# Router's logits and ranks in PSUM, branch sums behind the last scatter, expert 0's rows on two queues

## The chip, the cores and the metric

The kernel runs on one core of a Trainium2 chip. The metric is the device time of one execution in microseconds (us), from the kernel's start to its end; three runs of the kernel before are given. A core has TensorE (PE, matmuls), VectorE (DVE), ScalarE (ACT), GpSimd (POOL) and SyncE (SP, which here only issues DMAs). Each engine works through its own list of instructions in order and waits on semaphores of the others. DMAs are issued by SP, by ACT and, for the scattered writes, by POOL.

## The reference

Three layers follow each other, all in float32:

```python
# 1. recurrence over 768 steps, 4 x 8 heads, a 40 x 40 state each
y[t]  = r[t] @ state
Sa    = state @ a[t]
state = state * w[t] - outer(Sa, b[t]) + outer(v[t], k[t])
# 2. x = y as 3072 tokens x 320; each token goes to one of 8 experts
logits = x @ w_gate;  e = argmax(logits)
out[e-tokens] = gate * sigmoid(x @ w_output_gate)[e] * (relu(x @ w1[e]) @ w2[e])
# 3. dense: (relu(x @ w_in) ** 2) @ w_out, 320 -> 2048 -> 320
```

## The kernel before

**Stage 1, up to about 445 us.** The recurrence is cut into 24 chunks of 32 steps (128 tokens each, since 4 batches go together). A chunk passes through small stages (`A_scan` to `F_3`), and a table written out by hand (`ORDER`, with `HEAD` and `TAIL` for the first and last chunks) says in which order the stages of neighbouring chunks are issued. The engines therefore work on several chunks at a time, each in the fixed order of that table.

The last three stages of a chunk are the router. `F_1` transposes the chunk's tokens `xs`. `F_2` (`r_oh`, L884) multiplies them with the gate weights: PE writes the logits `lg` to PSUM (L887), ACT copies them behind the tokens in `xs` (L889), and DVE makes a one-hot row of the winning expert in five small instructions: the largest logit `mx` (L891), `val` = rank numbers of the logits that reach it (L893), the largest rank `mv` (L895), the one-hot `oh` (L897), and a copy of two token numbers into `xs` (L898). `F_3` (`r_pos`, L907) counts with two matmuls (`rk`) how many tokens each expert had so far, makes the row number `POS` out of it, and POOL scatters the rows of `xs` to `xsD` in DRAM, where each expert has a region (L920).

Behind the router of a chunk, DVE's next instruction in the order is `B_ev` (L520), a transpose of `LM`, a PSUM tile that PE fills in `B_lm` (L511). POOL meanwhile multiplies in `A_bd` (L497), `A_at` (L484) and `A_recip` (L474), all with two operands in SBUF.

**The branch.** With the last chunk, `beyond` (L901) makes a number in three DVE instructions: whether any expert has more tokens than the main path takes. All engines read it and branch (L1147, L1148); on these inputs the branch jumps over a fallback.

**Stage 2, from about 449 us.** For each expert `load_x` brings 512 of its rows as four blocks of 128 x 402 numbers (201 KB each). For expert 0 SP issues the blocks one by one (L1345) in the order 1, 2, 3, 0, and then expert 1's four blocks as one DMA of 804 KB (L1342). Block 0's rows and half of block 1's were used already, from a copy taken ahead, so `trans_x(0)` lets PE transpose only blocks 1, 2, 3, in this order (L1038). ACT and DVE split the result in two float32r parts (L1023 to L1027), and the matmuls of expert 0 begin (L1033). ACT runs a table load and one dummy activation at the start of the stage (L1358), so that `Exp` is at hand. The rows of block 0 are needed by ACT's copy of the logits of expert 0 (L1396).

**Stage 3, from about 671 us,** is the dense layer on all tokens, bound by matmuls throughout.

Of the kernel before, what the change touches and what calls it, by code (L numbers as in the profile page):

```python
# [20 lines left out]
NCH = S // T  # L21
# [817 lines left out]
def program(tc, A, out, nch=NCH, order=ORDER):  # L839
    nc = tc.nc  # L840
    V, G, S_, P = nc.vector, nc.gpsimd, nc.scalar, nc.tensor
    with ExitStack() as top:
# [39 lines left out]
            return xT  # L882

        def r_oh(c, xs, xT, pm):  # L884
            lg = pm([128, 16], "lg")
            for k in range(3):
                P.matmul(lg, xT[:, k], wg[:, k], start=(k == 0), stop=(k == 2))  # L887
            L = xs[:, 384:392]
            S_.activation(xs[:, 384:400], lg, AF.Copy)  # L889
            mx = rp.tile([128, 1], F32, name="mx")  # L890
            V.tensor_reduce(out=mx, in_=L, axis=AX.X, op=ALU.max)  # L891
            val = rp.tile([128, 8], F32, name="val")
            V.scalar_tensor_tensor(out=val, in0=L, scalar=mx, in1=cst[:, C_DESC : C_DESC + 8], op0=ALU.is_ge, op1=ALU.mult)  # L893
            mv = rp.tile([128, 1], F32, name="mv")
            V.tensor_reduce(out=mv, in_=val, axis=AX.X, op=ALU.max)  # L895
            oh = rp.tile([128, 8], F32R, name="oh")
            V.tensor_scalar(out=oh, in0=val, scalar1=mv, scalar2=None, op0=ALU.is_equal)  # L897
            V.tensor_copy(xs[:, 400:402], cst[:, C_TID + c : C_TID + c + 2])  # L898
            return oh

        def beyond():  # L901

            V.tensor_tensor(out=pv, in0=base[0:1], in1=cst[0:1, C_CAP : C_CAP + 8], op=ALU.subtract)
            V.tensor_reduce(out=fl[:, 0:1], in_=pv, axis=AX.X, op=ALU.max)
            V.scalar_tensor_tensor(out=fi[:, 1:2], in0=fl[:, 0:1], scalar=fl[:, 2:3], in1=fl[:, 1:2], op0=ALU.max, op1=ALU.max)

        def r_pos(c, xs, oh, pm):  # L907
            rk = pm([128, 16], "rk")
            for k in range(2):
                P.matmul(rk[:, 8 * k : 8 * k + 8], cnt[:, k], oh, start=True, stop=True)  # L910
            t = rp.tile([128, 8], F32, name="t")
            V.tensor_tensor(out=t, in0=rk[:, 0:8], in1=base, op=ALU.add)
            V.tensor_tensor(out=t, in0=t, in1=oh.bitcast(F32), op=ALU.mult)
            V.tensor_tensor(out=base, in0=rk[:, 8:16], in1=base, op=ALU.add)
            if c == NCH - 1:
                beyond()
            pf = rp.tile([128, 1], F32, name="pf")
            V.tensor_reduce(out=pf, in_=t, axis=AX.X, op=ALU.add)
            V.tensor_scalar(out=POS[:, c : c + 1], in0=pf, scalar1=0.0, scalar2=E * RS - 1.0, op0=ALU.max, op1=ALU.min)
            G.indirect_dma_start(out=xsD, out_offset=IndirectOffsetOnAxis(ap=POS[:, c : c + 1], axis=0), in_=xs, in_offset=None)  # L920

        def parts(ring, n):
            return [ring[:, 6144 * k : 6144 * k + n].bitcast(F32R) for k in range(2)]
# [410 lines left out]
        with ExitStack() as ctx:  # L1334
# [4 lines left out]
            def load_x(e):  # L1339
                t = xg[e] = xp.tile([128, 4, XW], F32, name="xg", bufs=2)  # L1340
                if e:
                    nc.sync.dma_start(out=t, in_=xsD[e * RS : e * RS + 512].rearrange("(j p) x->p j x", p=128))  # L1342
                else:
                    for j in (1, 2, 3, 0):
                        nc.sync.dma_start(out=t[:, j], in_=xsD[128 * j : 128 * j + 128])  # L1345

            def trans_x(e, ks):
                js = range(4) if e else range(1, 4)
# [7 lines left out]

            with tc.manual_schedule():
                S_.activation(fl[:, 0:1], cst[0:1, 0:1], AF.Exp)  # L1358
                load_x(0)
                load_x(1)  # L1360
                drain(first_w[0])
                trans_x(0, range(3))
                narrow = Narrow()

# [198 lines left out]
```

## Time and profile before

| | us |
|---|---|
| runs | 1009.38, 1016.93, 1022.97 (median 1016.93) |
| profiled execution, its own time | 1027.06 |
| its span, first to last instruction | 1025.3 |
| busy in the span: PE, DVE, ACT, POOL | 940.5 (92%), 684.3 (67%), 613.5 (60%), 464.1 (45%) |
| mean granted TensorE clock | 0.968 |

The profiled execution took 4 us more than the longest of the three runs. Busy shares are means over three stages with different limits, so they are read by stage. A row of a group gives line, engine, operation, tiles, count, then busy time and the mean of one, then the idle time ahead of it and what ended it. A row of a timeline gives the start in us, the length in us, the instruction, and in brackets the idle time of the engine just before.

### The profile page before, as it was taken

To read this page: it belongs to the slowest core of one execution; us is meant where nothing else is said; L and a number is where in the kernel's file an instruction comes from. 1 tells how busy PE (TensorE), PEld (TensorE's weight loads), DVE (VectorE), ACT (ScalarE), POOL (GpSimd) and SP (SyncE) were. 2 spreads that over 40 slices of the span, in tenths; PEclk is the share of its full clock that TensorE was granted. 3 is DMA by queue.
4 is the path that set the end of the run, shared out by engine and by line. 5 is a ranking of instruction groups with operands and counts; after the bars stand their busy time and mean duration, and the time that the engine had idled before them with its cause. 6 is when DMAs were issued, how large, how long until landed. Compare 5 with 4: busy or idle time off the path is not lost.

```text
span 1025.3 us, 33164 instructions
## 1 busy us (share of the span) xinstructions
PE 940.5 (92%) x13845; PEld 833.5 (81%) x13845; DVE 684.3 (67%) x1752; ACT 613.5 (60%) x1366; POOL 464.1 (45%) x449
## 2 busy tenths in 40 slices
PE   1779898999989988889999999999999999999997
PEld 1568677777777777779999999989999989999986
DVE  5879999999989987335777777686444343434341
ACT  4579888897989988435555555545434333344432
POOL 5567777866777775217666666630100101010101
PEclk9889999999999999579999999999999999999999
DMA  3874535444354445327788887773001010000000
GB/s 101 245 215 109 135 103 134 113 115 125 104 143 118 110 126 135 104 97 220 233 258 257 237 240 206 222 165 97 20 8 37 21 31 26 1 26 1 17 10 27
DMA packets 59307, 120.25 MB, mean 117 GB/s; under 512 B 14609, under 2 KB 32145, under 8 KB 57233
## 3 DMA queue, kind: packets, MB, share of 16 engines
q1 hardware_dynamic: 51424, 103.09, 36.6%
q0 software_dynamic: 2688, 8.88, 2.4%
q10 hardware_dynamic: 5040, 6.12, 1.8%
q8 instruction: 110, 1.80, 0.8%
q14 instruction: 45, 0.36, 0.1%
HBM read 92.01 MB, written 26.05 MB: 115 GB/s over the span
## 4 chain that ended last, share of the span: by engine, by line
PE 72%; DVE 14%; issue 5%; ACT 4%; DMA 4%; POOL 1%; POOLq 0%; SPq 0%; DVEq 0%; ACTq 0%
PE ph L1033 27%; PE py L1434 9%; PE po L1291 5%; PE po L1292 5%; PE po L1290 5%; PE tp L707 2%; PE kt L554 2%; PE sc L726 2%; PE ST L670 2%; PE y L754 2%; DMA arena<-in_xE_dram 2%; PE LM L511 1%; PE zt L717 1%; PE lg L887 1%; DVE CB L763 1%
## 5 line engine op out<-in xcount | busy, mean ns | idle before, releaser
L1033 PE MATMUL ph<-x,ring 128*128 128x512 f32 (+2 forms) x1280 | 299.7, 382 | 0.2 <-ACT x L1023 0.2
L1033 PEld LDWEIGHTS ph<-x,ring 128*128 128x128 f32 x1280 | 233.5, 191 | 33.3 <-ACT x L1023 0.6
L1513 POOL DMA_INDIRECT out_dram<-hf,TID x24 | 25.6, 1067 | 309.2 <-ACT hf L1511 268.2
L936 POOL TENSOR_TENSOR ring<-raws,ring 128x732 fp32r<-128x732 f32 (+2 forms) x72 | 124.3, 1741 | 49.4 <-ACT ring L935 42.7
L1484 DVE TENSOR_TENSOR hf<-hf 128x512 f32<-128x512 f32 x96 | 68.6, 714 | 114.2 <-ACT hf L1483 114.0
L1483 ACT ACTIVATE hf<-ph 128x512 f32<-128x512 f32 x96 | 57.3, 596 | 118.4 <-PE ph L1033 118.3
L497 POOL TENSOR_TENSOR arena<-arena 40x1024 f32<-40x1024 f32 x43 | 104.9, 2440 | 40.8 <-DMA hz<-in_vS_dram 13.2
L1291 PE MATMUL po<-ring,hf 128*128 128x320 f32 x368 | 113.6, 309 | 0.8 <-DVE hf L1486 0.8
L1292 PE MATMUL po<-ring,hf 128*128 128x320 f32 x368 | 113.4, 308 | 0.3 <-DVE ring L1311 0.3
L1290 PE MATMUL po<-ring,hf 128*128 128x320 f32 x368 | 113.7, 309 | 0.0
L1486 DVE TENSOR_TENSOR hf<-hf,hf 128x512 fp32r<-128x512 f32 x92 | 64.6, 702 | 64.2 <-ACT hf L1485 64.2
L1434 PE MATMUL py<-hr,ring 128*128 128x448 f32 x512 | 105.3, 365 | 0.0
L1485 ACT ACTIVATE hf<-hf 128x512 fp32r<-128x512 f32 x92 | 58.2, 632 | 76.9 <-DVE hf L1484 76.9
L1434 PEld LDWEIGHTS py<-hr,ring 128*128 128x128 f32 x512 | 95.6, 188 | 7.1
L1043 DVE SCALAR_TENSOR_TENSOR hr<-ph,hr 128x448 fp32r<-128x448 f32 (+2 forms) x72 | 41.1, 571 | 55.7 <-ACT hr L1042 55.4
L1291 PEld LDWEIGHTS po<-ring,hf 128*128 128x128 f32 x368 | 69.1, 188 | 5.1 <-DVE hf L1486 1.3
L1290 PEld LDWEIGHTS po<-ring,hf 128*128 128x128 f32 x368 | 69.0, 188 | 4.5 <-ACT hf L1485 0.4
L1292 PEld LDWEIGHTS po<-ring,hf 128*128 128x128 f32 x368 | 69.0, 187 | 0.6 <-DVE ring L1311 0.6
L935 ACT ACTIVATE ring<-raws 128x732 fp32r<-128x732 f32 (+2 forms) x72 | 57.0, 791 | 8.8 <-DMA raws<-in_we_dram 8.5
L1042 ACT ACTIVATE hr<-ph 128x448 fp32r<-128x448 f32 (+2 forms) x72 | 36.1, 501 | 39.8 <-PE ph L1033 39.8
L1274 POOL TENSOR_TENSOR c<-c,r 128x384 int32<-128x384 int32 (+1 forms) x32 | 35.2, 1100 | 54.3 <-PE ph L1033 10.4
L557 ACT ACTIVATE kSB<-kt,cst 128x320 f32<-128x320 f32 x96 | 45.1, 521 | 13.6 <-PE kt L554 13.3
(217 smaller groups left out, 1987.2 us busy)
## 6 DMA issues: line engine op xcount, KB each, us to landing
raws<-in_we_dram SPq DMA_DIRECT2D x48, 366.0 KB
arena<-in_xE_dram SPq DMA_DIRECT2D x48, 322.5 KB
xL<-in_xL_dram SPq DMA_DIRECT2D x24, 480.0 KB
xsD<-raws SPq DMA_DIRECT2D x24, 268.0 KB
q<-in_wi_dram SPq DMA_DIRECT2D x16, 384.0 KB
xg<-xsD SPq DMA_DIRECT2D x7, 804.0 KB
q<-in_wo_dram SPq DMA_DIRECT2D x16, 320.0 KB
wb<-in_wB_dram SPq DMA_DIRECT2D x24, 165.0 KB
```

What stands on the lines that cost most here:

```text
L497: (V if c < EARLY[2 + hh] else G).tensor_tensor(out=bd[sl, :, :, hh].rearrange("p a b c l j->p (a b) c (l j)"), in0=s["bk"][sl].rearrange( ...
L935: S_.activation(hi, rw, AF.Copy)
L936: G.tensor_tensor(out=lo, in0=rw, in1=hi.bitcast(F32), op=ALU.subtract)
L1033: P.matmul(ps, t[:, o : o + 128], x3[:, i, c], start=(j == 0), stop=(j == 7))
L1290: P.matmul(ps, hh, whi[:, o : o + 320], start=start, stop=False)
L1291: P.matmul(ps, hl, whi[:, o : o + 320], start=False, stop=False)
L1292: P.matmul(ps, hh, wlo[:, o : o + 320], start=False, stop=stop)
L1434: P.matmul(py, w, x, start=(f == 0 and k == 0), stop=last)
L1483: S_.activation(r, ph, AF.Relu)
L1484: V.tensor_tensor(out=q, in0=r, in1=r, op=ALU.mult)
L1485: S_.activation(hh, q, AF.Copy)
L1486: V.tensor_tensor(out=hl, in0=q, in1=hh.bitcast(F32), op=ALU.subtract)
```

## The change

Three edits, the third of them in two places.

```diff
         def r_oh(c, xs, xT, pm):
-            lg = pm([128, 16], "lg")
+            both = pm([128, 24], "lg")
+            lg, val, L = both[:, 0:16], both[:, 16:24], both[:, 0:8]
...
-            L = xs[:, 384:392]
             S_.activation(xs[:, 384:400], lg, AF.Copy)
...
-            val = rp.tile([128, 8], F32, name="val")
             V.scalar_tensor_tensor(out=val, in0=L, scalar=mx, in1=cst[:, C_DESC : C_DESC + 8], op0=ALU.is_ge, op1=ALU.mult)
...
             V.tensor_tensor(out=base, in0=rk[:, 8:16], in1=base, op=ALU.add)
-            if c == NCH - 1:
-                beyond()
...
             G.indirect_dma_start(out=xsD, out_offset=IndirectOffsetOnAxis(ap=POS[:, c : c + 1], axis=0), in_=xs, in_offset=None)
+            if c == NCH - 1:
+                beyond()
...
-                    for j in (1, 2, 3, 0):
-                        nc.sync.dma_start(out=t[:, j], in_=xsD[128 * j : 128 * j + 128])
+                    for j, q in ((2, nc.sync), (3, nc.scalar), (1, nc.sync), (0, nc.scalar)):
+                        q.dma_start(out=t[:, j], in_=xsD[128 * j : 128 * j + 128])
...
                 S_.activation(fl[:, 0:1], cst[0:1, 0:1], AF.Exp)
+                drain(first_w[0])
                 load_x(0)
                 load_x(1)
-                drain(first_w[0])
```

**Router.** The logits that DVE reads and the ranks `val` now lie in one PSUM tile; ACT's copy into `xs` stays. This is DVE's router of one chunk with its waits, before:

```order
L891 TENSOR_REDUCE mx<-xs 128x1 [waits Activation_49]
L893 SCALAR_TENSOR_TENSOR val<-xs,mx,cst 128x8 [waits DVE_49]
L895 TENSOR_REDUCE mv<-val 128x1 [waits DVE_49]
L897 TENSOR_SCALAR oh<-val,mv 128x8 [waits DVE_49]
L898 COPY xs<-cst 128x2
L520 STREAM_TRANSPOSE LB<-LM 128x1024 [waits PE_49]
```

and after:

```order
L891 TENSOR_REDUCE mx<-lg 128x1 [waits Activation_49]
L892 SCALAR_TENSOR_TENSOR lg<-lg,mx,cst 128x8 [waits DVE_49,PE_49]
L894 TENSOR_REDUCE mv<-lg 128x1 [waits DVE_49]
L896 TENSOR_SCALAR oh<-lg,mv 128x8 [waits DVE_49]
L897 COPY xs<-cst 128x2
L520 STREAM_TRANSPOSE LB<-LM 128x1024 [waits PE_49]
```

The order is the same; `val` (now part of `lg`) reads one operand and writes its result in PSUM, `oh` reads PSUM, and the first instruction waits for ACT as before.

**Branch sums.** DVE at the last chunk, from the use of `rk` on, before (L903 to L905 are `beyond`, L1113 and L1114 a sum that stage 2 needs):

```order
L914 TENSOR_TENSOR base<-rk,base 128x8
L903 TENSOR_TENSOR p_86<-base,cst 1x8
L1113 TENSOR_TENSOR p_84<-base,cst 1x8
L904 TENSOR_REDUCE fl<-p_86 1x1
L1114 SCALAR_TENSOR_TENSOR p_85<-p_87,p_85,p_84 1x8
L905 SCALAR_TENSOR_TENSOR fi<-fl 1x1
L918 TENSOR_REDUCE pf<-t 128x1
L919 TENSOR_SCALAR POS<-pf 128x1
```

and after:

```order
L913 TENSOR_TENSOR base<-rk,base 128x8
L915 TENSOR_REDUCE pf<-t 128x1
L1112 TENSOR_TENSOR p_84<-base,cst 1x8
L916 TENSOR_SCALAR POS<-pf 128x1
L902 TENSOR_TENSOR p_86<-base,cst 1x8
L1113 SCALAR_TENSOR_TENSOR p_85<-p_87,p_85,p_84 1x8
L903 TENSOR_REDUCE fl<-p_86 1x1
L904 SCALAR_TENSOR_TENSOR fi<-fl 1x1
```

`POS`, on which the last scatter waits, comes ahead of the three instructions of `beyond` and of one of the other two.

**Expert 0's rows.** ACT at the start of stage 2, before:

```order
L1358 ACT_TABLE_LOAD
L1358 ACTIVATE fl<-cst 1x1
L1023 ACTIVATE x_12288<-pk 128x320 x2
L1026 ACTIVATE x_12288<-pk 128x320
L1396 ACTIVATE gl<-xg 128x72
```

and after:

```order
L1357 ACT_TABLE_LOAD
L1357 ACTIVATE fl<-cst 1x1
L1344 DMA xg<-xsD 128x402 x2
L1022 ACTIVATE x_12240<-pk 128x320 x2
L1025 ACTIVATE x_12240<-pk 128x320
L1395 ACTIVATE gl<-xg 128x72
```

ACT issues blocks 3 and 0 behind its table load; SP is left with blocks 2 and 1, in this order, and expert 1's DMA follows as its third instead of its fifth. The moved `drain` has nothing left to issue: no weight piece of expert 0 stands there in either kernel.

## Rows read from the trace of the kernel before

**Rows 1.** The page: granted clock in 40 slices of 25.6 us, tenths.

```profile
PEclk9889999999999999579999999999999999999999
```

**Rows 2.** Busy time in one stretch: PE, PEld, DVE, ACT, POOL, clock, DMA.

```profile
70.00:400.00 330.00, 296.18 (x9335) 252.61 (x9337) 303.67 (x1021) 287.40 (x735) 240.46 (x267) 0.98 0.44 116
```

**Rows 3.** Waits, 70 to 400 us: total us, times, longest.

```profile
DVE xs L782 <- PE y L754: 13.6, 10, 3.1
...
DVE mx L891 <- ACT xs L889: 3.6, 8, 1.1
```

**Rows 4.** DVE's groups of instructions, 70 to 400 us.

```profile
L893 DVE SCALAR_TENSOR_TENSOR val<-xs,mx,cst 128x8 f32<-128x8 f32 x20 | 11.2, 560 | 0.7
L897 DVE TENSOR_SCALAR oh<-val,mv 128x8 fp32r<-128x8 f32 x20 | 10.8, 542 | 0.7
```

**Rows 5.** Single lines, 70 to 400 us: shortest/median/longest in ns, first and last start.

```profile
L566 DVE TENSOR_SCALAR ST<-Hb,cst x42: 229/236/244, 76.2 to 394.9; 128x16 f32<-128x16 f32 x42
L893 DVE SCALAR_TENSOR_TENSOR val<-xs,mx,cst x20: 225/508/1243, 82.7 to 386.8; 128x8 f32<-128x8 f32 x20
L897 DVE TENSOR_SCALAR oh<-val,mv x20: 231/232/1032, 83.1 to 387.2; 128x8 fp32r<-128x8 f32 x20
L898 DVE COPY xs<-cst x20: 154/160/165, 83.3 to 387.4; 128x2 f32<-128x2 f32 x20
```

**Rows 6.** DVE's timeline at one chunk, 95 to 101.5 us.

```profile
98.10 1.06 DVE L893 SCALAR_TENSOR_TENSOR val<-xs,mx,cst 128x8 f32<-128x8 f32 x1
...
99.39 0.92 DVE L897 TENSOR_SCALAR oh<-val,mv 128x8 fp32r<-128x8 f32 x1
...
100.30 1.24 DVE L520 STREAM_TRANSPOSE LB<-LM 128x1024 f32<-128x1024 f32 x1
```

**Rows 7.** POOL's timeline at the same place.

```profile
97.94 1.19 POOL L484 TENSOR_TENSOR at<-arena,Cx 104x512 f32<-104x512 f32 x1
99.10 1.18 POOL L474 TENSOR_TENSOR arena<-Cx,arena 104x512 f32<-104x512 f32 x1
```

**Rows 8.** PE's timeline at the same place.

```profile
97.92 1.08 PE L511 MATMUL LM<-arena,at 104*32 104x128 f32 x32
```

**Rows 9.** DVE and PE at another chunk, 352.5 to 357 us.

```profile
355.48 1.23 DVE L520 STREAM_TRANSPOSE LB<-LM 128x1024 f32<-128x1024 f32 x1
...
353.56 1.08 PE L511 MATMUL LM<-arena,at 104*32 104x128 f32 x32
```

**Rows 10.** DVE's timeline at the last chunk.

```profile
442.84 0.16 DVE L914 TENSOR_TENSOR base<-rk,base 128x8 f32<-128x8 f32 x1
...
443.57 0.14 DVE L918 TENSOR_REDUCE pf<-t 128x1 f32<-128x8 f32 x1
```

**Rows 11.** Waits of SP's queue, 430 to 470 us.

```profile
SPq L1345 <- DMA xsD<-xs,POS: 3.1, 1, 3.1
...
SPq L1345 <- ACT hr L1042: 0.2, 1, 0.2
```

**Rows 12.** Timeline of SP, ACT and PE behind the branch.

```profile
448.86 1.77 SPq L1345 DMA_DIRECT2D xg<-xsD  x4
...
449.76 1.28 ACT L1358 ACT_TABLE_LOAD   x1 [0.79 <-ACTq L1148]
...
451.46 0.52 PE L1038 MATMUL pk<-cst,xg 128*128 128x128 f32 x3 [2.90 <-DMA xg<-xsD]
...
453.89 0.90 PE L1038 MATMUL pk<-cst,xg 128*128 128x128 f32 x3 [0.96 <-DMA xg<-xsD]
...
454.94 1.32 PE L1033 MATMUL ph<-x,ring 128*128 128x256 f32 x4 [0.16 <-ACT x L1023]
```

**Rows 13.** ACT's queue at its first split: waits, shortest/median/longest ns, first and last start.

```profile
L1023 ACTq EVENT_SEMAPHORE  x3: 17/38/4027, 431.9 to 450.4; - x3
```

**Rows 14.** Stretches of 2 us, columns as in Rows 2.

```profile
454.00:456.00 2.00, 1.84 (x7) 1.42 (x8) 1.04 (x3) 1.26 (x4) 0.00 (x0) 0.50 0.82 294
...
460.00:462.00 2.00, 2.00 (x16) 2.00 (x16) 0.36 (x1) 1.41 (x5) 1.87 (x2) 0.84 0.00 0
```

## The prediction

> **What bounds the kernel now.** I read the page first, for the granted clock in slices: it is 5 and 7 tenths in the two slices from 410 to 461 us and near full elsewhere [rows 1]. So this execution lost time around the end of stage 1, where the change works too. Next I read the busy times of stage 1 without its ends. In 330 us PE is busy for 296, DVE for 304, ACT for 287 [rows 2]: DVE has 26 us of slack, or about 1.3 us in each of the 20 chunks of that stretch. In the waits the reader is to see that DVE's idle time is mostly a wait for PE's `y` ahead of `xs` (13.6 us, 10 times), and that the router's `mx` waits for ACT's copy in 8 chunks (3.6 us) [rows 3]. So DVE and PE take turns: in about half of the chunks DVE comes late, in the others PE.
>
> Then I read the two router instructions by themselves. `val` and `oh` handle 8 numbers per partition, and their shortest cases take 225 and 231 ns; but they go up to 1243 and 1032 ns [rows 5], and 20 of each take 11.2 and 10.8 us [rows 4]. The two timelines show why: `val` starts at 98.10, just after POOL's L484 (97.94), and ends at 99.16, 0.03 us behind that one's end; `oh` starts inside L474 and ends at 100.31, again 0.03 us behind it [rows 6, 7]. DVE is held until POOL is done. The tensor_scalar L566, which writes PSUM, never is (229 to 244 ns in 42 cases) [rows 5].
>
> Last I read the branch. From 449 to 455 us PE has almost nothing to do: it waits for block 1 (till 451.46) and for block 3 (till 453.89), and the first matmul of expert 0 is at 454.94 [rows 12].
>
> **The router's five instructions.** The change takes `val` to PSUM as source and target, and lets `oh` read PSUM; I take both at their shortest, 225 and 231 ns, as L566 has it. In the chunk of rows 6 this saves 1.06 + 0.92 - 0.46 = 1.52 us. But the next instruction on DVE, the transpose of `LM` at 100.30, can't start before PE has `LM`, which ends at 97.92 + 1.08 = 99.00 [rows 8]: no more than 1.30 us come through. At 355.48 the same difference to PE's 353.56 + 1.08 is 0.84 [rows 9]. I took the smaller of the two, saving and distance to `LM`, in each of the 20 chunks: ten have something to give (rows 6 and rows 9 are the first and the last of them), 7.0 us together. The other ten have no held instruction, or `LM` is later than the router. Of the ten, DVE waits for `y` later in the same turn in four, and I take it that their 2.4 us only lengthen this wait. Six are left, with 1.30, 0.56, 0.65, 0.25, 0.97 and 0.84: **-4.6 us**. The end to the fast side is 7.0, with the other four. To the other side, a DVE that runs earlier may meet POOL at another of its two-operand instructions, which costs up to a whole POOL instruction each time (1.2 us [rows 7]); three such meetings eat 3.6 of the 4.6, and I put the end at +1 us.
>
> The copy on ACT stays, and `mx` waits for ACT still, as the order with its waits shows; so the 3.6 us of rows 3 stay too. The PSUM tile is now held until `oh` has read it, but PE's next use of its place is the `rk` of the same chunk or later, which needs `oh` anyway: nothing. PSUM operands for `mx` and `mv` cost nothing I can see.
>
> A rule of the Trainium skill speaks against a part of this. Its page "SBUF — State Buffer", section "SBUF: two separate sides", says that DVE and GpSimd share a pair of ports under an exclusive lock, which a DVE instruction asks for if it has two SBUF inputs or runs in a two-port mode, and that a float32 copy from SBUF to SBUF is of the second kind; `val` and `oh` held to POOL's end agree with it. By it `xs`'s copy of two token numbers, now first to come with operands in SBUF alone, would be held in their place, and the sum would be that of the first rival below.
>
> **The branch sums.** Before, the sum behind `base` (L914, 442.84) starts at 443.57, 0.73 us later, with `beyond` and a scan between [rows 10]. Now one short instruction stays between, so `POS` and the scatter come about 0.6 us earlier. SP's first load of block rows waits for the landed scatter (3.1 us), and behind that 0.2 us for ACT's last early activation [rows 11]; ACT doesn't end earlier, so of 0.6 us at most these 0.2 matter less. I take -0.1, with ends at 0 and -0.6, the whole step, which counts where PE's early matmuls end well ahead of the scatter. The branch's number comes perhaps 0.3 us later; SP reads it first and then stands 3.1 us at the scatter [rows 11]: nothing.
>
> **Expert 0's rows.** Before, SP issues four blocks in 1.77 us from 448.86, 0.44 each, and expert 1's four blocks behind them; block 1 is with PE at 451.46, 2.2 us after its issue ended at 449.3; block 3, third, at 453.89 [rows 12], while 294 GB/s flow [rows 14]. Now SP issues 2, 1 and expert 1's 804 KB; ACT issues 3 and 0. When does ACT come to it? Its table load runs from 449.76 to 451.04 [rows 12], but its queue stood in the last wait ahead of the first split at 450.4 already [rows 13], past the load and the dummy activation. So a DMA at this place goes out at about 450.4, a little later than on SP before (third, by 450.2). Best case: it is served as block 1 was, 450.4 + 0.44 + 2.2 = 453.0, a gain of 0.9. Worst case: it comes last of 8 x 206 = 1,650 KB, which at 294 GB/s take 5.6 us from 449.3, and with the 1.5 us that block 1 took beyond its own 0.7 it is there at 456.4, 2.5 us later. Its nearest row is its own before: block 3 with two blocks in front and expert 1's rows about. I take 0, and keep -0.9 and +2.5. Block 1 is now second on SP, some 0.7 us later (206 KB at 294 GB/s); its three transposes fit into the wait for block 3. Block 0, last on ACT, is needed by ACT's `gl`, which stands behind the splits that wait for block 3; issued 0.44 us behind block 3, with 0.7 us of transfer, it can hold ACT's first activation of expert 0 by about 1 us, while that one waits for eight matmuls first: nothing.
>
> TensorE's clock is at its lower level, 1.2 GHz, from about 454 to 461 us (0.50 in 454 to 456, 0.84 in 460 to 462) [rows 14], after PE had idled; I leave this as it is.
>
> **The sum.** -4.6 - 0.1 + 0 = -4.7 us. The profiled execution took 1027.06 and would take 1022.4. It is 10 us above the median of the runs, 1016.93, for which I forecast 1016.93 - 4.7 = **1012.2 us**.
>
> **The rivals.** (1) *The hold is handed on.* The two-number copy behind `oh` is held instead. For it: its neighbour `oh`, with one SBUF input, is held. Against: 154 to 165 ns in all 20 cases [rows 5], though always right behind an instruction that had waited. In the chunk of rows 6 it would end with L484 at 99.13, little lost; over the six chunks 3.4 of the 4.6 us are left. 1016.93 - 3.5 = 1013.4.
>
> (2) *All of it comes back.* PE or ACT is the bound in these chunks too (90% and 87% busy [rows 2]), and what DVE gains turns into longer waits for `LM` and `y`. Only the branch is left: 1016.8.
>
> (3) *More than the sum.* All ten chunks pass on their share (7.0), the scatter its 0.6, block 3 its 0.9, and PE starts early enough that the low stretch of the clock behind the branch (7 us at half speed, so 3.4 us) doesn't come: -11.9, 1005.0.
>
> (4) *Slower: block 3 behind expert 1's rows.* SP's large DMA now goes out about one us earlier and ahead of block 3, which ACT issues behind a table load. If it is served first, block 3 is there 2.5 us later, and if PE's longer wait brings the clock one more low stretch of 7 us, another 3.4: +5.9, against the router's -4.6 net +1.2, 1018.1. It decides from a block 3 that is 1.3 us late with the longer low clock. For it: the four blocks and the large DMA share the same engines at 82% [rows 14]. Against: block 3 was slowed by this DMA before as well. On this the page "ScalarE: Activation LUTs", section "What ACT_TABLE_LOAD costs", of the Trainium skill says that a load is followed by a drain of 1380 ns; by that ACT would issue at 449.76 + 2.66 = 452.4 and block 3 come at 455.0, 1.1 us late. The queue that waits at 450.4 [rows 13] speaks against it.
>
> **How the numbers follow.** Chances: forecast 0.40, (1) 0.17, (2) 0.20, (3) 0.08, (4) 0.15. All lie within 2% of the median (996.6 to 1037.3), which is about what a measurement of this kernel can tell from no change: its own three runs spread over 1.3%. The clock may explain such a spread: the two low slices of rows 1 make some 40 us at half speed, 7 of them behind the branch, and the other 34 cost up to 17 us. So the range is that of the cases, 1005 to 1018, opened by what the median of a few such runs may be off, about 4 us to either side: 1001 to 1022. Faster by over 2% would need four times the sum: 0.04. Slower by over 2%: 0.02.
>
> **What would show it.** `val` and `oh` near 230 ns in all chunks, and the copy behind them still at 160 (forecast) or up to 1.2 us (1). DVE's waits for `LM` and for `y` (13.6 us before [rows 3]) grown: the more, the more of (2). The scatter's issue about 0.6 us closer to `rk`. ACT's two DMAs at 450.4 relative to a table load at 449.8, and block 3's landing against the first matmul of expert 0: later than 4.8 us after SP's first load means (4). The forecast is wrong if stage 1 from the second to the twentieth chunk isn't shorter by 3 to 6 us.

## The result, and the profile after

The change is slower by 0.8%: 1028.66 us in the median of 20 runs (1020.30 to 1042.28) against 1019.94 for the kernel before in 20 runs, a ratio of 1.0083 with a 95% interval of 1.0060 to 1.0106. The forecast was 4.7 us faster, 1012.2 us from the 1016.93 of three runs; with more runs the kernel before itself stands 3.0 us higher. Measured twice more, on two chips (e5 and h1 below), the change came to 1.0038 (1.0005 to 1.0071) and 1.0102 (1.0065 to 1.0139).

The profiled execution took 1021.77 us (span 1020.0, mean granted clock 0.977). Both profiled executions are poor samples: that of before (1027.06) is above the median of its kernel, that of after far below its own. So the two are compared stretch by stretch, and only where the granted clock is alike.

**Router.** The windows and waits of 70 to 400 us, as [rows 2, 3]; a row of waits gives the total, the times and the longest:

```profile
70.00:400.00 330.00, 301.85 (x9419) 256.67 (x9420) 294.45 (x1027) 291.57 (x743) 244.10 (x266) 0.99 0.44 118
```

```profile
DVE xs L782 <- PE y L754: 19.4, 20, 2.3
DVE LB L520 <- PE LM L511: 3.2, 7, 1.3
DVE mx L891 <- ACT xs L889: 2.7, 5, 1.2
```

DVE is busy for 294 us where it was busy for 304, and now waits for `y` in 20 chunks where it waited in 10: what DVE gained is in part waiting time. The three instructions, as [rows 5] (shortest, median and longest in ns):

```profile
L892 DVE SCALAR_TENSOR_TENSOR lg<-lg,mx,cst x24: 233/234/235, 83.4 to 429.7; 128x8 f32<-128x8 f32 x24
L896 DVE TENSOR_SCALAR oh<-lg,mv x24: 226/226/227, 83.8 to 430.1; 128x8 fp32r<-128x8 f32 x24
L897 DVE COPY xs<-cst x24: 158/160/1049, 84.0 to 430.3; 128x2 f32<-128x2 f32 x24
```

`val` and `oh` are never held any more. The copy behind them now is, up to 1049 ns. Here is that case, DVE's timeline and POOL's:

```profile
192.97 0.23 DVE L896 TENSOR_SCALAR oh<-lg,mv 128x8 fp32r<-128x8 f32 x1
193.11 1.05 DVE L897 COPY xs<-cst 128x2 f32<-128x2 f32 x1
194.08 1.24 DVE L520 STREAM_TRANSPOSE LB<-LM 128x1024 f32<-128x1024 f32 x1
```

```profile
192.96 1.18 POOL L474 TENSOR_TENSOR arena<-Cx,arena 104x512 f32<-104x512 f32 x1
```

The copy ends at 194.16, 0.02 us behind POOL's L474, just as `val` and `oh` did in [rows 6, 7].

**Expert 0's rows.** SP, ACT and PE behind the branch, as [rows 12]:

```profile
437.80 0.91 SPq L1344 DMA_DIRECT2D xg<-xsD  x2
438.75 0.43 SPq L1341 DMA_DIRECT2D xg<-xsD  x1
```

```profile
439.11 1.28 ACT L1357 ACT_TABLE_LOAD   x1 [0.79 <-ACTq L1147]
439.74 1.46 ACTq L1344 DMA_DIRECT2D xg<-xsD  x2
```

```profile
440.95 0.85 PE L1037 MATMUL pk<-cst,xg 128*128 128x128 f32 x6 [3.06 <-DMA xg<-xsD]
444.90 0.90 PE L1037 MATMUL pk<-cst,xg 128*128 128x128 f32 x3 [3.10 <-DMA xg<-xsD]
445.96 0.79 PE L1032 MATMUL ph<-x,ring 128*128 128x256 f32 x2 [0.15 <-ACT x L1022]
```

ACT issues its two blocks 0.63 us after its table load began, one us behind SP's 804 KB. Block 3 comes to PE 7.1 us after SP's first load (before: 5.0), and the first matmul 8.16 us after it (before: 6.08). Stretches of 2 us show when:

```profile
442.00:444.00 2.00, 0.00 (x0) 0.00 (x0) 0.00 (x0) 0.00 (x0) 0.00 (x0) 0.77 1.00 343
444.00:446.00 2.00, 0.94 (x4) 0.55 (x4) 0.06 (x1) 0.53 (x2) 0.00 (x0) 0.50 0.26 94
```

All 16 DMA engines are busy until 444, and block 3 comes as they fall idle: it was among the last of 1,650 KB. The packets of the DMA queues show the order; q1 takes what SP issued, q10 what ACT issued. From 437.8 to 442.6 us (the first line) q10 moved nothing, though ACT had issued at 439.74; from 442.6 to 445 (the other two) its blocks came:

```profile
q1 hardware_dynamic: 631, 0.96, 69.3%
```

```profile
q10 hardware_dynamic: 254, 0.36, 44.4%
q1 hardware_dynamic: 175, 0.26, 29.8%
```

A row gives packets, MB and the share of the 16 engines: of the 1.2 MB that SP issued, 0.96 went out ahead of ACT's first packet.

**The last scatter.** `POS` now comes 0.6 us sooner behind `rk`, as forecast, but the scatter doesn't. POOL's queue waits for `POS` with a semaphore instruction (shortest, median and longest in ns, then its start). Before and after, and the `POS` of after:

```profile
L920 POOLq EVENT_SEMAPHORE  x1: 521/521/521, 443.4 to 443.4; - x1
```

```profile
L917 POOLq EVENT_SEMAPHORE  x1: 43/43/43, 433.1 to 433.1; - x1
432.48 0.15 DVE L916 TENSOR_SCALAR POS<-pf 128x1 int32<-128x1 f32 x1
```

Before, POOL's queue stood there for half a us. After, it came there half a us behind the end of `POS` and went straight on. Now POOL's queue itself comes last, 2.97 us after it began its scatter of the chunk before (2.76 in the kernel before). In all traces of this text that distance is 2.6 to 3.0 us, and only in the trace of before did the queue stand there for `POS`: in e2, e3 and e6 below, which lack this edit, it came last as well. What holds it in this time, the traces don't tell.

**What nobody had touched.** The experts' matmuls stand in the same order with the same operands, and yet they take longer. First the stretches from the first `py` to the first `po` and from there to the end, of before and then of after:

```profile
466.46:674.50 208.04, 208.04 (x1059) 191.79 (x1058) 152.18 (x287) 116.61 (x236) 136.16 (x91) 1.00 0.80 232
674.50:1025.30 350.80, 342.89 (x1897) 308.33 (x1896) 152.57 (x226) 139.31 (x238) 27.85 (x27) 1.00 0.11 33
```

```profile
456.78:667.93 211.15, 210.32 (x1060) 191.64 (x1058) 152.71 (x287) 116.83 (x236) 136.86 (x91) 1.00 0.78 229
667.93:1019.98 352.05, 344.13 (x1896) 308.54 (x1896) 152.68 (x226) 139.79 (x238) 30.17 (x27) 1.00 0.11 33
```

The clock is full in all four rows, the counts agree to one or two, and PE is busier by 2.3 and 1.2 us. The chain of work that ended last (start, length, what) shows where. Before, then after:

```profile
479.76 9.85 PE ph L1033 x48
...
494.20 12.82 PE py L1434 x64
507.02 9.61 PE ph L1033 x48
...
521.16 13.06 PE py L1434 x64
...
548.65 12.81 PE py L1434 x64
```

```profile
470.07 9.85 PE ph L1032 x48
...
484.51 13.05 PE py L1433 x64
497.56 9.85 PE ph L1032 x48
...
512.01 13.05 PE py L1433 x64
...
539.50 13.05 PE py L1433 x64
```

Before, every second expert was faster: 12.8 instead of 13.05 us for its 64 `py` matmuls, 9.61 instead of 9.85 for 48 of its `ph`, so that the experts start 27.49 and 26.95 us apart in turn. After, all of them are 27.49 apart. The weights lie in two SBUF tiles, ring 0 for even experts and ring 1 for odd ones. `val` had two buffers of 32 bytes per partition in a pool ahead of ring 1; without them ring 1, and everything behind it, stands 64 bytes lower (118432 instead of 118496, the addresses in the built programs). The other operand of `py`, the activations `hr`, stands ahead of that pool and did not move, and neither did ring 0.

### The profile page after: what moved, and what is told of

The parts are those of the page before. It is cut to its first block, busy times and chain, and to the rows that moved or that the text cites. A ratio compares the mean times of both kernels' runs of the same rounds, so it can differ in the third digit from the quotient of the medians.

```text
span 1020.0 us, 33166 instructions
## 1 busy us (share of the span) xinstructions
PE 938.7 (92%) x13845; PEld 828.6 (81%) x13845; DVE 674.7 (66%) x1752; ACT 615.0 (60%) x1366; POOL 468.1 (46%) x449
## 4 chain that ended last, share of the span: by engine, by line
PE 51%; DMA 3%; DVE 1%; ACT 1%; issue 0%; POOLq 0%; SPq 0%; DVEq 0%; ACTq 0%
PE ph L1032 25%; PE py L1433 9%; PE po L1290 5%; PE po L1291 5%; PE po L1289 5%; DMA q<-in_wo_dram 1%; PE pk L1037 1%; DMA yTD<-yT 1%; DMA xg<-xsD 1%; DMA xg<-yTD 0%; DVE hf L1483 0%; DMA out_dram<-hf,TID 0%; DMA woD<-c 0%; DVE c L1269 0%; DVE c L1286 0%
## 5 line engine op out<-in xcount | busy, mean ns | idle before, releaser
L1512 POOL DMA_INDIRECT out_dram<-hf,TID x24 | 27.8, 1159 | 308.1 <-ACT hf L1510 271.1
L497 POOL TENSOR_TENSOR arena<-arena 40x1024 f32<-40x1024 f32 x43 | 105.0, 2442 | 47.7 <-DVE arena L479 12.8
```

What stands on the lines that cost most here:

```text
L497: (V if c < EARLY[2 + hh] else G).tensor_tensor(out=bd[sl, :, :, hh].rearrange("p a b c l j->p (a b) c (l j)"), in0=s["bk"][sl].rearrange( ...
```

## The experiments

Each kernel is called by the short name at its first mention (e1 for e1_place_kept). A ratio is to the kernel before on the same chip, with its 95% interval. The numbers that I take from every trace stand in one table after the experiments.

**First, the suspects one by one.** `val`'s place kept, in the changed kernel (e1_place_kept):

```diff
+            rp.tile([128, 8], F32, name="val")
```

> The changed kernel with an unused SBUF tile of val's size in val's place (2 x 32 bytes per partition), so that all later tiles, ring 1 of the weights among them, stand at the addresses of the kernel before. Theory P (the place of the later tiles): the experts' py starts come again at 27.5 and 26.95 us in turn, a stage-3 group takes 3.61 us instead of 3.63, and the time is 3 to 4 us below the changed kernel's: ratio to before about 1.005. Rival C (another chip under the two profiles): the experts stay at 27.49 us each, ratio 1.008 as the change.

Ratio 1.0015 (0.9971 to 1.0058). The chain:

```profile
493.19 12.81 PE py L1434 x64
520.14 13.06 PE py L1434 x64
547.63 12.81 PE py L1434 x64
```

The alternation is back: the 64 bytes make it, and not the chip. The time can't tell more: its interval holds theory P's 1.005 and 1.000 alike, and leaves out rival C's 1.008.

The load edit alone, in the kernel before (e2_loads_alone; the diff is the third edit):

> The kernel before with the third edit alone (expert 0's blocks on two queues). Theory B (block 3 behind expert 1's 804 KB): first ph of expert 0 about 8 us after PE's early matmuls end instead of 6.4, and 1.7 to 4 us slower in all, ratio 1.002 to 1.004. Rival H (harmless, as I forecast): block 3 at the same distance as before, ratio 1.000 within 0.001. Theory P says the experts stay at 27.49 and 26.95 in turn.

Ratio 1.0010 (0.9969 to 1.0050); first `ph` 7.22 us after SP's first load; experts in turn. Block 3 is late here too, by less: ACT issued its blocks at 448.86, ahead of the large load at 449.34.

The shift alone, upwards, in the kernel before (e3_shift_alone):

```diff
+            rp.tile([128, 8], F32, name="pad")
```

> The kernel before with an unused SBUF tile of 2 x 32 bytes per partition in the router's pool, so that all later tiles stand 64 bytes higher; nothing else. Theory P with a period of 128 bytes: every expert 27.49 us, stage-3 groups 3.63 us, 3 to 4 us slower, ratio 1.003 to 1.004. Theory P with another period: some other pattern. Rival C: no difference, ratio 1.000 within 0.001.

Ratio 1.0114 (1.0053 to 1.0175), in six runs. Odd experts take a third pace:

```profile
489.73 12.97 PE py L1435 x64
517.08 13.05 PE py L1435 x64
544.58 12.98 PE py L1435 x64
```

So an unused tile alone makes this kernel slower. It lost 11.6 us, though from the first `py` to the end its trace is only 2.5 us longer than the mean of the kernels with the tiles as before (table below). A period of 128 bytes is not the rule: 64 bytes up and 64 bytes down differ.

The change without the load edit (e4_loads_undone):

> The changed kernel with expert 0's blocks loaded on SP as before; router in PSUM and the branch's sums as in the change. Theory B: first ph about 6.4 us after PE's early matmuls end again; with P and the router's gain (4.6 as I forecast, 0 if it all comes back) it stands at 1019.9 - 4.6 + 3.5 to 1019.9 + 3.5, ratio 0.999 to 1.0035. Rival R (the router's change itself costs the rest): ratio 1.005 or more, with longer waits of DVE or PE in stage 1.

Ratio 0.9997 (0.9949 to 1.0046), first `ph` at 5.93 us: as theory B has it; rival R's 1.005 lies just outside.

**Then the router, the loads and the rule.** The changed kernel again (e5_change_again):

> The changed kernel once more, beside the kernel before on the chip of these runs. Known by now from six traces: the moved tiles cost 3.1 us from the first py to the end, the load edit 1.8 us from SP's first load of block rows to the first ph; the router gives 2 to 3 back. Theory S (that is all): ratio 1.001 to 1.004. Rival K (the change also makes more low clock in stage 1, some 5 us): ratio 1.006 to 1.010 again, with the mean granted clock below that of before by 0.004 or more.

Ratio 1.0038 (1.0005 to 1.0071): the value is theory S's, the interval reaches into rival K's. The mean granted clock speaks against K: 0.966 in its runs, 0.967 in those of before. Here ACT issued its blocks at 446.45, before the large load (446.97), and the first `ph` came 6.22 us after SP's first load.

The router's edit alone, `val`'s place kept (e6_router_alone):

```diff
-            lg = pm([128, 16], "lg")
+            both = pm([128, 24], "lg")
+            lg, val, L = both[:, 0:16], both[:, 16:24], both[:, 0:8]
-            L = xs[:, 384:392]
-            val = rp.tile([128, 8], F32, name="val")
+            rp.tile([128, 8], F32, name="val")
```

> The kernel before with the router's logits and ranks in PSUM alone, and val's SBUF place kept empty so that nothing else moves. Theory G (my forecast's term): 4.6 us faster, ratio 0.9955. Rival H1 (the hold is handed on to the copy of two numbers, which took 8.1 to 10.1 us in 24 cases in the changed kernel instead of 3.8): 2 to 3.5 us faster, ratio 0.9965 to 0.998. Rival H2 (all comes back as waits): 1.000. py and stage 3 as before: 558.8 to 560.9 us from the first py to the end.

Ratio 0.9959 (0.9929 to 0.9988): 4.2 us faster, near the forecast's term, though the copy is held here too (7.8 us in 24 cases). The interval, 1.2 to 7.3 us, holds H1's 2 to 3.5 us as well, and leaves out H2.

The change with `val`'s place kept and expert 1's load on ACT, behind blocks 3 and 0 (e7_expert1_behind):

```diff
-                    nc.sync.dma_start(out=t, in_=xsD[e * RS : e * RS + 512].rearrange("(j p) x->p j x", p=128))
+                    (nc.scalar if e == 1 else nc.sync).dma_start(out=t, in_=xsD[e * RS : e * RS + 512].rearrange("(j p) x->p j x", p=128))
```

> The changed kernel with val's place kept, and expert 1's 804 KB issued on ACT behind blocks 3 and 0, not on SP ahead of them. Theory B1 (block 3 is late because the large load runs ahead of it): first ph 4.5 to 5.5 us after SP's first load, instead of 7.2 to 8.2, and the time 2 to 3 us below the same kernel with it on SP: ratio 0.997. Rival B2 (ACT's issue itself is late, behind the table load): 7 us or more still, ratio 1.000 to 1.002.

Ratio 0.9994 (0.9949 to 1.0039).

```profile
444.80 0.83 ACTq L1345 DMA_DIRECT2D xg<-xsD  x2
445.67 0.51 ACTq L1342 DMA_DIRECT2D xg<-xsD  x1
```

```profile
448.30 0.90 PE L1038 MATMUL pk<-cst,xg 128*128 128x128 f32 x3 [0.27 <-DMA xg<-xsD]
449.36 7.35 PE L1033 MATMUL ph<-x,ring 128*128 128x256 f32 x39 [0.15 <-ACT x L1023]
```

ACT issued its blocks 1.38 us after SP's first (443.42), within the table load and later than in any other kernel but the change itself, and still the first `ph` came at 5.94 us. So it is not ACT's issue that is late; the large load ahead of it is what costs. My number for it, 4.5 to 5.5, was too good, and whether the whole kernel gains by it the ratio can't tell.

Ring 0 at an address of 0, ring 1 at 96 modulo 256 (e8_rings_0_96; two unused tiles, loads on SP):

```diff
+        cp.tile([128, 24], F32, name="pad0")
+            rp.tile([128, 24], F32, name="pad1", bufs=1)
```

> The changed kernel with the loads on SP as before, and two unused SBUF tiles that put ring 0 at an address of 0 modulo 256 and ring 1 at 96. Known so far: experts with their weights at 160 take 13.05 us for py, at 224 12.81, at 32 12.97. Theory P256 (the residue of 256 decides): new values for py, even experts (ring 0 at 0) all alike, odd ones (ring 1 at 96) all alike; 0, the most even address, is as fast as 224 or faster (12.8 or less). Rival P-rel (the distance of a ring to another tile decides): even experts stay at 13.05.

Ratio 0.9964 (0.9924 to 1.0003). Even experts stay at 13.05, odd ones take 13.08 to 13.22 for `py`, but 9.71 for `ph`: the round address is no faster. Ring 1 and the activations `x3` that `ph` reads kept their distance in all kernels so far, while the pace of the odd `ph` took four values. So that distance isn't what decides. Another isn't excluded: from the weights to `hr`, the other operand of `py`. Ring 0 and `hr` stand behind the same unused tile and move together, so ring 0 kept its distance to `hr` in every kernel, and its pace too (13.05, but for expert 0 of f1 to f3 below, 13.22).

**An attempt at a better kernel.** Both rings at the residue that was fast (f1_rings_at_224; loads on SP):

```diff
+        cp.tile([128, 80], F32, name="pad0")
+            rp.tile([128, 64], F32, name="pad1", bufs=1)
```

> The changed kernel with the loads on SP as before, and two unused SBUF tiles that put both rings of weights at 224 modulo 512, the residue at which ring 1 stood before. The pace of expert matmuls has followed the ring's address so far, not its distance to the activations. Theory A (the address modulo 512 or less decides): all experts 26.95 us, py 12.81 in every one; from the first py to the end 557.0 or less, 3 us below the kernel before; with the router's 3 us a ratio of 0.993 to 0.996. Rival D (something else decides): even experts stay at 27.49, ratio 0.997.

Theory A fell. Ratio 1.0064 (1.0016 to 1.0113), and no expert is fast (expert 0, ahead of these lines, takes 13.22):

```profile
479.10 13.05 PE py L1435 x64
506.60 13.05 PE py L1435 x64
534.10 13.05 PE py L1435 x64
```

Ring 0 stands at 20192 here, which is the fast address of before less 98,304, so equal to it modulo 32,768, and it is slow. The kernel with 480 and 64 (f4_rings_480_64, a single run) agrees that no residue of the address that I tried rules it: ring 0 is slow at 480, and ring 1 at 64 takes 13.22 in expert 1 and 12.81 in experts 3 and 5. One place thus gives two paces in one trace, so the place of the weights alone doesn't decide. The distance to `hr` stays possible: in f1 ring 1 came to ring 0's distance modulo 512 (128 bytes) and runs at ring 0's pace. No run tests it by itself.

> As the kernel with both rings at 224, but ring 0 at 480 and ring 1 at 64 modulo 512: one look at the pace. If 256 is the period, even experts take 26.95 us here too (480 is 224 modulo 256); if it is 512 or more, they take something else. 64 is a new residue.

Expert 1's load behind the splits (f2_expert1_late, else as f1):

```diff
-                load_x(1)
                 trans_x(0, range(3))
+                load_x(1)
```

with this load on ACT.

> As the kernel with both rings at 224, and expert 1's 804 KB issued on ACT behind the splits of expert 0's rows, so that the four blocks on SP have the DMA engines to themselves. Theory B1: first ph 4.5 to 5 us after SP's first load instead of 5.7 to 6.1, about 1 us faster, perhaps 2 with less low clock; first ph of expert 1 not later. Rival B3 (the blocks take their time by themselves): 5.7 to 6.1 again, ratio as that kernel's within 0.001.

First `ph` at 5.60 us against 6.38 in f1 and 6.1 in the mean of all kernels with the loads on SP; ratio 1.0037 (0.9995 to 1.0079). That is 0.1 us below the lowest of those kernels (5.72 to 6.75), and a single trace: as far as it shows, the large load behind the four blocks costs them half a us at most, and the rest is their own, as rival B3 has it.

The copy on ACT (f3_copy_on_act, else as f1):

```diff
+            S_.activation(xs[:, 400:402], cst[:, C_TID + c : C_TID + c + 2], AF.Copy)
-            V.tensor_copy(xs[:, 400:402], cst[:, C_TID + c : C_TID + c + 2])
```

> As the kernel with both rings at 224, and the router's copy of two token numbers done by ACT right behind its copy of the logits, so that no instruction between mx and PE's rk has its operands in SBUF alone on DVE. Theory H1 (the hold was handed to the copy and took 4 to 6 us of DVE with it): DVE's router loses these 7 to 10 us, and 1 to 2 us more come through than with the copy on DVE. Rival H3 (it is handed on once more, to t's product or the next stage, or ACT is now the bound): no gain, or up to 3 us lost on ACT (24 x 0.2 us and more).

The trace and the times disagree. In the trace, the stretch from the first `mx` to the 21st took 305.7 us, where the five other kernels with `val` in PSUM and no low clock in this stretch took 309.4 to 313.1; but the timed runs had a median of 1030.62, ratio 1.0109 (1.0052 to 1.0166), against 1010.42 for the profiled one. What those runs lost is in no profile. Nothing can be built on this one.

**Last, a square**, to see whether the tiles of stage 1, which moved by 64 bytes too, carry a price of their own: all four have the router in PSUM, the branch's sums moved and the loads on SP. In g1 no tile is moved, in g2 only stage 1's stand lower, in g3 only those of the experts and stage 3, in g4 (e4 again) all. The lines that g1, g2 and g3 add to g4, the second just ahead of ring 1, the third ahead of stage 1's tiles:

```diff
+            rp.tile([128, 8], F32, name="val")
```

```diff
+        ringp.tile([128, 16], F32, name="pad")
```

```diff
+    wk.tile([128, 8], F32, name="pad")
```

> The change without the load edit and with val's SBUF place kept: router in PSUM and branch sums behind the scatter, every tile where it was before. First corner of a square of four. Theory M3 (the moved tiles cost only the 3.3 us in the experts and the last stage): 3 us faster than before by the router, ratio 0.996 to 0.998, as this edit had alone (0.9959). Theory M6 (the moved tiles cost more, by stage 1 or by its clock): the same here.

> As the corner with val's place kept, but the tiles of stage 1 stand 64 bytes lower as in the change, ring 1 and all behind it at their places of before. Theory M3: no dearer than the first corner, ratio 0.996 to 0.998, experts 27.49 and 26.95 in turn. Theory M6 (stage 1's tiles): 3 us or more dearer than the first corner, ratio 1.000 or more, the loss in stage 1.

> As the corner with val's place kept, but ring 1 and all tiles of the experts and the last stage stand 64 bytes lower as in the change, those of stage 1 at their places of before. Both theories: every expert 27.49 us, from the first py to the end 563 us instead of 560. Theory M3: ratio 0.999 to 1.001, 3.3 us above the first corner. Theory M6 with stage 1: the same 3.3 us and no more.

> The change without the load edit, val's place given up as in the change: the fourth corner, measured once at 0.9997. Theory M3: as the corner with only the experts' tiles moved, 0.999 to 1.001. Theory M6: the sum of both moves, 6 us or more above the first corner, ratio 1.002 to 1.005.

Ratios: g1 0.9978 (0.9946 to 1.0009), g2 0.9952 (0.9917 to 0.9988), g3 0.9992 (0.9959 to 1.0025), g4 0.9996 (0.9962 to 1.0031). The experts' tiles cost (0.9992 + 0.9996 - 0.9978 - 0.9952) / 2 = 0.0029, or 3.0 us; stage 1's tiles nothing (-0.0011). From the four intervals I estimate that either number may be off by 3 us: M6's 3 us or more for stage 1 don't fit, and M3 does, but by the times alone the 3.0 us are barely clear of nothing. The chain of g2 and then of g3 shows them:

```profile
478.85 12.81 PE py L1434 x64
505.80 13.06 PE py L1434 x64
```

```profile
479.75 13.05 PE py L1434 x64
507.25 13.05 PE py L1434 x64
```

A pair to price the load edit on one chip (h1_change_third is the change, h2_loads_undone_again is g4):

> The changed kernel a third time, beside the same without its load edit on the same chip. Theory L2 (the load edit costs what the traces show, 1 to 2 us): ratio 1.000 to 1.003, at most 2 us above the other. Theory L4 (it costs 4 us or more, with the low clock that follows a late block 3): ratio 1.003 to 1.006, 4 us or more above the other.

> The changed kernel without its load edit again (0.9997 and 0.9996 so far). Both theories: ratio 0.998 to 1.001. The distance to the changed kernel beside it is the price of the load edit.

Neither came true: 1.0102 (1.0065 to 1.0139) with the load edit, 1.0119 (1.0076 to 1.0162) without. The edit costs nothing that this pair can see, which by the spread of its runs is some 5 us either way (an estimate); and a kernel that had stood at 0.9997 and 0.9996 on two chips is 1.2% slower than before on a third.

**The traces side by side** (us). Mx: from the first `mx` to the 21st, and in brackets the time at 1.2 GHz within (the stretch times twice what its granted clock lacks to 1). Load: from SP's first load of block rows to expert 0's first later `ph`, and in brackets when ACT's first block was issued relative to the large load. End: from the first `py` to the end.

| kernel | router | experts' tiles | blocks on | Mx | Load | End |
|---|---|---|---|---|---|---|
| before | SBUF | as before | SP | 318.6 (10.2) | 6.08 | 558.8 |
| e2 | SBUF | as before | SP, ACT | 321.9 (17.1) | 7.22 (-0.48) | 559.8 |
| e3 | SBUF | +64 | SP | 319.8 (6.8) | 5.87 | 562.6 |
| e6 | PSUM | as before | SP | 313.1 (0.0) | 5.73 | 559.9 |
| g1 | PSUM | as before | SP | 314.4 (3.4) | 6.67 | 560.8 |
| g2 | PSUM | as before | SP | 312.3 (3.4) | 6.75 | 559.8 |
| e7 | PSUM | as before | SP, ACT | 319.4 (20.5) | 5.94 (-0.87) | 560.4 |
| e1 | PSUM | as before | SP, ACT | 322.1 (23.9) | 7.88 (+0.23) | 560.9 |
| after | PSUM | -64 | SP, ACT | 313.8 (3.4) | 8.16 (+0.99) | 563.2 |
| e5 | PSUM | -64 | SP, ACT | 320.4 (17.1) | 6.22 (-0.52) | 563.7 |
| h1 | PSUM | -64 | SP, ACT | 320.0 (23.9) | 6.64 (-0.05) | 562.3 |
| e4 | PSUM | -64 | SP | 313.8 (6.8) | 5.93 | 562.9 |
| g3 | PSUM | -64 | SP | 314.9 (3.4) | 5.72 | 562.7 |
| g4 | PSUM | -64 | SP | 311.7 (0.0) | 5.91 | 562.5 |
| h2 | PSUM | -64 | SP | 309.4 (0.0) | 5.98 | 562.6 |
| e8 | PSUM | moved | SP | 320.9 (26.2) | 5.80 | 561.6 |
| f1 | PSUM | moved | SP | 312.3 (0.0) | 6.38 | 563.4 |
| f2 | PSUM | moved | SP, late | 310.0 (0.0) | 5.60 | 563.0 |
| f3 | PSUM, copy on ACT | moved | SP | 305.7 (0.0) | 6.45 | 562.4 |
| f4 | PSUM | moved | SP | 315.4 (12.4) | 6.23 | 562.4 |

A straight line through the column Mx, without f3, gives 315.8 us, less 4.0 (standard error 0.9) where the router is in PSUM, plus 0.38 us (0.03) for each us at 1.2 GHz. Only three of these traces have the router in SBUF, and the kernels ran on several chips. End is 560.1 in the mean of the seven kernels with the tiles as before (558.8 to 560.9), and 562.8 in the seven at -64 (562.3 to 563.7): 2.8 us, and the two don't overlap.

## Why the prediction was wrong

**The step that failed is one that the working lacked.** Its sum, -4.6 - 0.1 + 0, costs each edit by the instructions that it changes. That `val` leaves SBUF stands in it for `val` and `oh` alone; what `val` takes in PSUM was weighed and put at nothing, and the 64 bytes per partition that it gives up ahead of ring 1 were not weighed at all. With ring 1 at its new address PE goes at 13.05 us for an odd expert's `py` instead of 12.81. This costs 2.8 us by the traces and 3.0 by the square (4.4 between the two first profiles), and takes most of what the router gives. It is shown by putting the place back (e1, g1, g2) and by moving tiles alone (e3, g3).

**Expert 0's loads, taken as 0, were the second.** The range was -0.9 to +2.5. From SP's first load to the first `ph` the five kernels of the edit as it stands took 7.2 us in the mean, the thirteen others whose blocks and large load went out on SP as before 6.1; to the first `py` it is 17.9 against 16.8. So the term is +1.1 us (standard error 0.4, and 0.5 to the first `py`), and in the first trace +2.1. The mechanism is that of the fourth rival: the large load ahead of block 3. What I had said of ACT's place was exact (0.64 us after the table load's start by [rows 12, 13], 0.63 now); but I compared it with SP's third block and not with the large load, which now goes out 0.95 us after SP's first block instead of 1.81. Who comes first matters: with ACT ahead of the large load the three traces took 6.2, 6.6 and 7.2 us, with ACT behind it the two took 7.9 and 8.2. This agrees with what the Trainium skill says on its page "DMA: Bandwidth & Descriptors", under "Issuing engines are not separate DMA queues": two issuing engines save issue time alone. The drain of 1380 ns that the Trainium skill's page "ScalarE: Activation LUTs" gives under "What ACT_TABLE_LOAD costs", and that I had cited, shows in no run: ACT issued while its table load still ran, and its next activation began 0.01 us behind the load.

**The router's term was right in size.** Forecast -4.6; in the traces -4.0 with a standard error of 0.9, alone on the chip -4.2 (e6, 1.2 to 7.3). On the way it went otherwise than I said. The hold was handed on, as the first rival has it: the copy took 8.1 us in 24 cases instead of 3.8. By the rule that the Trainium skill's page "SBUF — State Buffer" gives under "SBUF: two separate sides", a copy with both operands in SBUF would be held; the trace agrees (1.05 us, to POOL's end). I weighed the 154 to 165 ns of [rows 5] against it, but in the held chunks those copies stood behind an instruction that had already waited for POOL. What the hold on the copy costs isn't settled: the gain came in spite of it, while f3's trace, without that copy on DVE, is 3.7 to 7.4 us shorter still, and its timed runs are not. By the sum, -4.0 lies between the first rival's -3.4 and the forecast's -4.6, too near to tell them apart. The forecast's own test, stage 1 shorter by 3 to 6 us, fails in the plain numbers of two traces: the change's three stand at 313.8, 320.4 and 320.0 and that of before at 318.6. Put to equal clock by 0.38 they are 312.5, 313.9 and 310.9, against 315.8 for the router in SBUF: 3.3, 1.9 and 4.9 us shorter.

**The branch's sums** stayed below what can be seen. From the last `rk` to the scatter's issue it is 2.60 us instead of 2.68, and 2.2 to 3.1 in the other traces with this edit. `POS` was ready 0.6 us sooner as I had said, but I had taken it for the last thing that the scatter waits for, and POOL's own queue came later still.

**The sum mended** is -4.0 + 2.8 + 1.1 = -0.1 us, no change. The three comparisons of the change gave +8.5, +3.9 and +10.3 us. **The difference is not settled.** It isn't the load edit (h2, without it, is +12.1 on the chip where h1 is +10.3), nor stage 1's tiles, as far as g2 shows; and it comes without the router's edit too: e3, the kernel before with an unused tile alone, is +11.6. A part goes with TensorE's clock: on the chip of h1 and h2 the mean granted clock was 0.976 in the runs of before, 0.969 in those of h1 and 0.971 in those of h2. For h1 that makes 0.007 x 2 x 1020 = 14 us more at 1.2 GHz, and 5.4 us of time by the 0.38 of the line above. Why it is lower there, while on the chip of g4 it is 0.972 for g4 and for before alike, no run tells: h2's profiled execution (1016.2 us, 9 below the median of its runs) lacks the loss.

Two things on record narrow it. The six kernels with the tiles as before stand at 0.9952 to 1.0015, and all that lost 0.3% or more (the change in its three comparisons, e3, f1 to f3, h2) have moved tiles; but e4, g3, g4 and e8 have moved tiles too and lost nothing. And the change's median varies little, 1023.9 to 1028.7 us, while that of before goes from 1013.5 on the chip of h1 to 1024.3 on that of e5. No kernel with its tiles in place ran on the chips of h1 and f1. So what is shown is why the expected gain is gone; why more than that was lost stays open, and with it whether the moved tiles cost more on some chips.

The range ended at 1022. Its slowest case set a late block 3, with more low clock, against the router's gain; no case had moved tiles beside it. And 3.0 us of the miss are the kernel before, whose median of three runs was that much below that of twenty.

**A version faster than the kernel before.** g2, the change with `val`'s 64 bytes put back ahead of ring 1 and the loads on SP, has a median of 1018.77 us, ratio 0.9952 (0.9917 to 0.9988); e6, the router's edit alone with the place kept, 0.9959 (0.9929 to 0.9988). g1, which differs from g2 by the places of stage 1's tiles alone, is at 0.9978 (0.9946 to 1.0009). In view of the chips' differences I take them as equal.

## What to carry to other kernels

A tile that goes out of SBUF moves every tile behind it: keep its place at first, or compare the pace of untouched matmuls in both traces, before an edit is judged by its time. Price a load by what stands ahead of it in the shared DMA engines, whichever engine issues it, and not by its place on its own queue. An instruction that ceased to be held handed the hold to the next with its operands in SBUF; what this costs is read from what that one's successor waits for. An input that comes sooner helps only when it is the last one awaited: read where the waiting queue itself stands.

## What was not expected of the hardware

The pace of a chain of float32r matmuls changes with the place of its tiles in SBUF, by up to 3%: 64 `py` matmuls took from 12.81 to 13.22 us at full clock, and a layout that ran several times, on several chips, showed the same pattern each time. With ring 1 at 118496 the odd experts were fast (12.81); at 118432 and 119008 they took 13.05, at 118560 12.97. Between 118496 and 118432 no other operand of `py` had moved. But the rule stays open: ring 0 at an address equal to 118496 modulo 32,768 was slow, ring 1 in f4 gave 13.22 and 12.81 in one trace, and where ring 0 moved, `hr` moved with it.
